# Weighted sums of an attention kernel in half groups of columns, at three places in four steps

## The chip, the cores and the metric

The kernel runs on one core of one Trainium2 chip. The core has a matrix engine (TensorE, "PE" in the profile, its weight loads "PEld"), a vector engine (VectorE, "DVE"), a scalar engine (ScalarE, "ACT"), GpSimd ("POOL") and a sync engine that issues transfers ("SP"). Matrix products go to banks of an accumulator memory of 128 partitions, 512 float32 columns each. The metric is the time of one execution on the device, in microseconds (us); lower is better. Times are medians of several executions; the profile is one execution.

## What is computed

One transformer-like block in float32 on x of 2048 rows and 512 columns. The rows are normalised; 32 query heads of 16 channels share one key and one value head; beside it stands a dense layer with Mish; the block's output is `x + s * g`.

```python
def _A_ref(x, wq, wk, wv, wo):
    q = ((x @ wq).reshape(B, S, H, Dh)).transpose(0, 2, 1, 3)
    k = x @ wk
    v = x @ wv
    scores = jnp.einsum("bhqd,bkd->bhqk", q, k) * (Dh ** -0.5)
    p = _softmax(scores, axis=-1)
    o = jnp.einsum("bhqk,bkd->bhqd", p, v)
    return o.transpose(0, 2, 1, 3).reshape(B, S, H * Dh) @ wo

def _B_ref(x, w1, b1, w2):
    h = jnp.einsum("bsd,df->bsf", x, w1) + b1
    act = h * jnp.tanh(softplus(h))
    return jnp.einsum("bsf,fd->bsd", act, w2)

xn = _layernorm(x, axis=-1)
s = _A_ref(xn, A_wq, A_wk, A_wv, A_wo)
g = _silu(_B_ref(xn, B_w1, B_b1, B_w2))
return x + s * g
```

## The kernel before

**Steps.** The attention is worked off in 512 steps. A unit `v` (there are 32) is four heads by 512 rows of queries, a block `k` (16 per unit) is 128 keys; step `s` stands for unit `s // 16`, block `s % 16`. A lead-in written as a small planner (tasks with times) does the normalisation, the keys and the first products; then the main loop runs 492 steps, and the last 20 (`LEAD`) go in pairs (`late_pair`). In the main loop each step issues to TensorE, in an order written out by hand:

- four score products `e` (`e_one`, L1098), each 64 rows of the array by 512 columns. ScalarE makes the exponential of each from the bank (L1100) into a buffer `pt`; there are `NPT` of these buffers, handed out in turn, and three banks `e`. A step fills buffers for one half of the array and two blocks, so that two neighbouring steps, an even one and the next, complete two blocks.
- four score products `m` (`m_one`, L1119) for a later unit, whose row maxima VectorE takes from the bank (L1123) into `mb`; there are three banks `m`. From the maxima `c_rows` makes the correction rows of a unit (`mp`, `cr`, once in 16 steps), which eight small transfers put beside the queries.
- half-array parts of one dense product group, `xs` in `waves` (L120, names `xps`): a group is a list of 12 or 15 products (queries, the Mish layer's first and second product, the output product), summed up in one bank.
- the weighted sum `pv` (L1187) of the block two steps back: `pv(s)` gives each of four 32-column tiles of the array its exponentials, 512 columns, with the 32-column values `vaug` as weights. It appears in the trace as eight products. After the 16th block of a unit `o_out` copies the bank out on ScalarE (L1196) and issues eight transfers.

**Halves of the array.** The products `e`, `m` and `xs` use one half of the array's rows, so that two run side by side as a pair. `waves` works a chunk of a group's products (six of twelve; eight or seven of fifteen; five where the steps allow it) first on one half `h` in one step and then on the other half in the next: a group of 12 or 15 takes four steps, or six with chunks of five. Both halves add into the same bank. `waves` keeps order between them by `cur["relay"]`: the ScalarE or VectorE instruction that was issued just behind the last x of a step; the first x of the group's next step is given a dependence on it ("other half of the bank"). A group's first step has none. After the group's last x, `finish` issues the evacuation of the bank (`xps` has one bank).

**Jobs.** The longer element-wise chains (Mish, SiLU, inverse of the softmax sums) go to ScalarE as jobs from a queue: `act_jobs(n)` issues one at the end of each step, two when over three wait, none (one when over three wait) where the step has evacuated on ScalarE. Between them GpSimd works at times counted in steps (`due`).

Of the kernel before, what the change touches and what calls it, by code (L numbers as in the profile page):

```python
# [42 lines left out]
HOLD = 1  # L43
STEP_US = 2.95
XMAX = 8
NPT = 15
EM = "MEMEMEME"
MLAG = 4
NHB = 4
# [77 lines left out]
def block_kernel(ctx: ExitStack, tc: tile.TileContext, x, wq, wk, wv, wo, w1, b1, w2, out):  # L127
# [97 lines left out]
            xin[c, tt] = sb.tile([P, D], F32, tag=tag, name=f"xin{c}_{tt}", bufs=n)  # L225
            sp.dma_start(xin[c, tt], xr[4 * c + tt])

    mvs = cp.tile([P, NKT, 2], F32, name="mvs")

    def stats(t):  # L230
        st = sb.tile([P, 6], F32, tag="st", name=f"st{t}")
        dve.bn_stats(st, xin[divmod(t, 4)])
        dve.bn_aggr(mvs[:, t], st)

    ve = cp.tile([P, NKT], F32, name="ve")
    hv = cp.tile([P, NKT], F32, name="hv")

    def stt(o, a, k, b, op0, op1):
        dve.scalar_tensor_tensor(o, a, k, b, op0=op0, op1=op1)  # L239
# [172 lines left out]
    def act_jobs(n):  # L412
        n = (int(len(jobs) > 3) if gap[0] else n) if n < 9 else n
        gap[0] = 0
        while n > 0:
            k = next((k for k, (fn, free) in enumerate(jobs)
                      if free is None or free() is not None and free() <= step[0]), None)
            if k is None:
                return
            fn = jobs[k][0]  # L420
            del jobs[k]
            fn()
            n -= 1
            ran[0] += 1
# [263 lines left out]
    def chunk_size(n, most):  # L688
        return -(-n // -(-n // most)) if n else 0

    def waves(h, em, new):

        if not cur["chunk"] and (not new or cur["g"] is None and not begin()):
            mms = []
        else:
            g = cur["g"]
            mms = cur["chunk"] or g.mms[cur["n"]:cur["n"] + chunk_size(len(g.mms) - cur["n"], g.most)]  # L700
        second = bool(cur["chunk"])
        k = len(mms)
        ms = em(k, second)
        a = deque(ms[1 - h])
        b = deque(ms[h])
        ps = cur["ps"]
        ends = second and cur["n"] + k == len(cur["g"].mms)
        xs = deque(mms)
        swap = k % 2 and k > 5 and not second
        relay = None  # L710
        first = True
        done = False
        while a or b or xs:
            if xs:
                i = xs.popleft().half(ps, h)
                if first and cur["relay"] is not None:
                    tc.add_manual_dep(i.ins, cur["relay"].ins.name, mybir.DependencyInfo(
                        mybir.DependencyClass.Sync, mybir.DependencyReason.DATA), reason="other half of the bank")
                first = False
                if ends and cur["g"].dve and len(xs) == HOLD + k % 2:  # L720
                    held[0] = []
                if not xs and ends:
                    cur["n"] += k
                    cur["chunk"] = []
                    finish()
                    done = True
                    for top in held[0] or ():
                        top()
                    held[0] = None
            elif b and not swap:  # L730
                b.popleft()()
            if len(a) > 1 or a and not xs:
                r = a.popleft()()
                if k and not xs and relay is None:
                    relay = r
            if b and swap and not xs and not a:
                b.popleft()()
        if k and not done:
            assert relay is not None
            cur["relay"] = relay  # L740
            if second:
                cur["n"] += k
                cur["chunk"] = []
            else:
                cur["chunk"] = mms
# [400 lines left out]

    def c_rows(v):

        mp = sb.tile([P, 2, 3, 8], F32R, tag="mp", name=f"mp{v}", bufs=2)
        mx = f(mp[:, :, 0])  # L1150
        w = {}

        def reduce():
            dve.reduce_max(out=mx, in_=mb_of[v].rearrange("p b (a z) -> p a z b", a=2), axis=AX.X)

        def high():
            dve.tensor_reduce(out=mp[:, :, 1], in_=mx.rearrange("p a (z o) -> p a z o", o=1), axis=AX.X,
                              op=ALU.max, negate=True)

        def low():  # L1160
            dve.tensor_reduce(out=f(mp[:, :, 2]), in_=f(mp[:, :, 0:2]).rearrange("p a s z -> p a z s"), axis=AX.X,
                              op=ALU.add, negate=True)

        def turn():
            cr = w["cr"] = sb.tile([P, 32], F32, tag="cr", name=f"cr{v}", bufs=2)
            dve.transpose(cr, f(mp[:, :, 1:3]).rearrange("p a s z -> p a (s z)"))

        def move():
            q, cr = qt_of[v], w["cr"]
            for a in range(1, -1, -1):  # L1170
                r = 64 * a + 48
                for b in range(4):
                    sp_at(0.68)
                    sp.dma_start(f(q[r:r + 2]).rearrange("o p (t b n) -> b o (p t) n", b=4, n=32)[b],
                                 cr[32 * b + 16 * a:32 * b + 16 * a + 16])
        return reduce, high, low, turn, move

    def pv(s):
        v, k = divmod(s, 16)
        if k == 0:  # L1180
            pv_of[v] = ps_v.tile([P, C], F32, tag="v", name=f"pv{v}")
        o = pv_of[v]
        for p in range(2):
            for a in range(2):
                pt = pt_of.pop((s, p, a))
                j = 2 * p + a
                pe.matmul(o[32 * j:32 * j + 32], vaug[:, k], pt, start=(k == 0), stop=(k == 15))  # L1187

    def o_out(v):
        c, g = divmod(v, 8)  # L1190
# [83 lines left out]
    def due(t):  # L1274
        step[0] = t
        for k in sorted(k for k in timed if k <= t):
            for fn in timed.pop(k):
                fn()
# [264 lines left out]
    rowq = deque()  # L1543
    pv_next = [0]

    def pv_to(s):

        while pv_next[0] <= s:
            k = pv_next[0]
            pv(k)  # L1550
            pv_next[0] += 1
            if k % 16 == 15:
                o_out(k // 16)
                return

    for s in range(NS + 2000):
        inm = s < NS - LEAD
        if inm or cur["chunk"]:
            assert s < NS
            due(s)  # L1560
            h = s % 2

            def em(k, second):
                n, rest = m_sides(1 - h, k, second) if inm else (0, 0)
                x = deque(lambda i=i: e_one(s, i) for i in range(4))
                y = deque(lambda: m_one(1 - h) for _ in range(n))
                r = [[], []]
                for op in EM if k % 2 == 0 or k == 5 or second else EM[::-1]:
                    if op == "M" and y:
                        r[1 - h].append(y.popleft())  # L1570
                    elif op == "E":
                        r[1 - h].append(x.popleft())
                r[h] = [lambda j=j: m_one(h, n + rest > 4 and j == rest - 1) for j in range(rest)]
                return r

            if s >= 2 and (s - 1) % 16 == 0 and s > 1:
                gap[0] += 1
            waves(h, em, s < NS - LEAD - 1)
            act_jobs(1 + (len(jobs) > 3))
            due(s + 0.5)  # L1580
            pv_to(s - 2)
        elif s < NS:
            due(s)
            if not late_banks:
                late_banks.extend(ps_m.tile([P, C], F32, tag="m", name=f"late{k}") for k in range(3))
                if (NS - s) % 2:
                    for i in range(4):
                        e_one(s, i)
                    fill(4)
                    act_jobs(1)  # L1590
                    pv_to(s - 2)
                    step[0] = s
                    continue
            if (NS - s) % 2 == 0:
                late_pair(s)
            else:
                if s < NS - 3:
                    act_jobs(1)
                pv_to(s - 1)
        else:  # L1600
            due(s)
            if s == NS:
                act_jobs(2)
                pv_to(NS - 1)
                due(s + 0.5)
                lanes_end()
                fill(3)
                fill(3)
            fill(16)
            act_jobs(100)  # L1610
        step[0] = s
        if vdone[0] < 8 * NC and min(m_next) >= m_need(vdone[0]):
            r = c_rows(vdone[0])
            rowq.extend([lambda r=r: (r[0](), behind.append(r[1])),
                         lambda r=r: (r[2](), behind.append(lambda: (r[3](), r[4]())))])
            vdone[0] += 1
        if rowq and not evacs[0]:
            rowq.popleft()()
        while behind and s >= NS - LEAD - 1:
            behind.popleft()()  # L1620
        evacs[0] = 0
        pump()
        if s > NS + 1 and not queue and cur["g"] is None and not timed and not jobs:
            break
# [12 lines left out]
```

## Time and profile before

| | |
|---|---|
| median of 3 runs | 1576.38 us (1576.18 to 1576.9) |
| the profiled execution | 1576.55 us |
| its span, first to last instruction | 1574.4 us |
| granted TensorE clock | 1.000 |
| instructions | 31742 |

A line of a group reads: line of the kernel, engine, operation, output<-inputs by the program's names, shape, count | busy us, mean ns of one | idle us of the engine ahead of them, and what released it. A line of a timeline reads: start in us, us taken, engine, line, operation, names, shape, count; in brackets the idle time ahead and its releaser. Consecutive instructions of one kind that overlap are merged. A matmul's duration is a latency: the next one may start earlier.

### The profile page before, as it was taken

To read this page: it belongs to the slowest core of one execution; us is meant where nothing else is said; L and a number is where in the kernel's file an instruction comes from. 1 tells how busy PE (TensorE), PEld (TensorE's weight loads), DVE (VectorE), ACT (ScalarE), POOL (GpSimd) and SP (SyncE) were. 2 spreads that over 40 slices of the span, in tenths; PEclk is the share of its full clock that TensorE was granted. 3 is DMA by queue.
4 is the path that set the end of the run, shared out by engine and by line. 5 is a ranking of instruction groups with operands and counts; after the bars stand their busy time and mean duration, and the time that the engine had idled before them with its cause. 6 is when DMAs were issued, how large, how long until landed. Compare 5 with 4: busy or idle time off the path is not lost.

```text
span 1574.4 us, 31742 instructions
## 1 busy us (share of the span) xinstructions
PE 1562.6 (99%) x11738; PEld 842.0 (53%) x11738; DVE 1341.1 (85%) x2329; ACT 1307.8 (83%) x2518; POOL 633.7 (40%) x683
## 2 busy tenths in 40 slices
PE   9999999999999999999999999999999999999998
PEld 5555555555555555555555555555555555555554
DVE  8998888889889888888998988888889998888832
ACT  7588788798998779878989887887898878789886
POOL 4774266284464105503515320471251515126412
PEclk9999999999999999999999999999999999999999
DMA  6243231232331314122032222211332213032020
GB/s 191 93 124 112 65 101 44 60 118 84 125 97 41 103 44 137 45 69 83 24 100 65 64 93 69 85 59 30 112 99 85 74 40 111 19 111 58 15 81 28
DMA packets 74666, 124.31 MB, mean 79 GB/s; under 512 B 21520, under 2 KB 35344, under 8 KB 74512
## 3 DMA queue, kind: packets, MB, share of 16 engines
q1 hardware_dynamic: 74512, 122.29, 25.2%
q8 instruction: 93, 1.52, 0.4%
q14 instruction: 61, 0.50, 0.1%
HBM read 74.78 MB, written 26.21 MB: 64 GB/s over the span
## 4 chain that ended last, share of the span: by engine, by line
PE 95%; DVE 4%; ACT 1%; DMA 0%; issue 0%; SPq 0%; ACTq 0%; DVEq 0%
PE xps L120 44%; PE pv L1187 32%; PE e L1098 9%; PE m L1119 7%; DVE mb L1123 3%; PE late L120 1%; PE xps L116 0%; ACT pt L1100 0%; DMA xin<-in_dram 0%; PE late L1098 0%; PE kp L351 0%; PE wop L120 0%; PE xp L302 0%; PE late L116 0%; PE wop L116 0%
## 5 line engine op out<-in xcount | busy, mean ns | idle before, releaser
L1123 DVE TENSOR_REDUCE mb<-m 128x1 f32<-128x512 f32 x2048 | 1274.2, 683 | 171.3 <-PE m L1119 152.3
L1100 ACT ACTIVATE pt<-e 128x512 f32<-128x512 f32 x2018 | 1061.6, 602 | 220.7 <-PE e L1098 212.3
L1119 PE MATMUL m<-ks,qt 48*128 48x512 f32 (+1 forms) x2048 | 829.9, 421 | 1.6 <-DVE ks L239 0.5
L1098 PE MATMUL e<-qt,ks 64*128 64x512 f32 x2018 | 740.4, 401 | 0.3
L1187 PE MATMUL pv<-pt,vaug 128*32 128x512 f32 x4096 | 543.0, 604 | 0.0
L1119 PEld LDWEIGHTS m<-ks,qt 48*128 48x128 f32 (+1 forms) x2048 | 372.9, 185 | 55.7 <-DVE mb L1123 18.5
L1098 PEld LDWEIGHTS e<-qt,ks 64*128 64x128 f32 x2018 | 373.3, 186 | 17.9 <-ACT pt L1100 7.5
L120 PE MATMUL xps<-wbs,act 64*128 64x512 f32 x1248 | 339.1, 408 | 0.2
L120 PEld LDWEIGHTS xps<-wbs,act 64*128 64x128 f32 x1248 | 217.7, 185 | 177.4 <-ACT pt L1100 105.8
L120 PE MATMUL xps<-xt,ws 64*128 64x512 f32 x1104 | 305.8, 410 | 0.1
L120 PEld LDWEIGHTS xps<-xt,ws 64*128 64x128 f32 x1104 | 190.6, 185 | 182.7 <-ACT pt L1100 116.5
L174 POOL TENSOR_SCALAR t<-t 128x512 f32<-128x512 f32 x56 | 34.4, 615 | 395.1 <-ACT t L838 394.9
L1187 PEld LDWEIGHTS pv<-pt,vaug 128*32 128x32 f32 x4096 | 81.9, 108 | 137.4 <-issue 129.1
L164 POOL TENSOR_TENSOR hb<-hb,t 128x512 f32<-128x512 f32 x56 | 72.1, 1287 | 65.6 <-ACT t L851 52.4
L120 PE MATMUL xps<-xt,wq 64*128 64x512 f32 x336 | 93.2, 410 | 0.0
L120 PEld LDWEIGHTS xps<-xt,wq 64*128 64x128 f32 x336 | 58.0, 185 | 55.2 <-ACT pt L1100 35.2
L120 PE MATMUL xps<-wbs,ot_all 64*128 64x512 f32 x288 | 79.5, 409 | 0.0
L120 PEld LDWEIGHTS xps<-wbs,ot_all 64*128 64x128 f32 x288 | 49.6, 185 | 46.7 <-ACT pt L1100 29.3
L164 POOL TENSOR_TENSOR hb<-hb,u 128x512 f32<-128x512 f32 x56 | 72.3, 1291 | 4.4
L164 POOL TENSOR_TENSOR u<-u,t 128x512 f32<-128x512 f32 x56 | 71.8, 1282 | 4.7
L164 POOL TENSOR_TENSOR act<-hb,act 128x512 fp32r<-128x512 f32 x55 | 70.8, 1288 | 4.6
L159 POOL TENSOR_SCALAR qh<-qf 128x512 fp32r<-128x512 f32 x15 | 9.3, 620 | 111.8 <-ACT qf L770 76.2
(158 smaller groups left out, 954.9 us busy)
## 6 DMA issues: line engine op xcount, KB each, us to landing
wbs<-w SPq DMA_DIRECT2D x36, 512.0 KB
ws<-w SPq DMA_DIRECT2D x35, 512.0 KB
qt<-qh SPq DMA_DIRECT2D x256, 32.0 KB
w<-wbs SPq DMA_DIRECT2D x14, 512.0 KB
wq<-wq SPq DMA_DIRECT2D x14, 512.0 KB
wbs<-wo SPq DMA_DIRECT2D x12, 512.0 KB
rawws<-in_dram SPq DMA_DIRECT2D x21, 256.0 KB
rawwb<-in_dram SPq DMA_DIRECT2D x20, 256.0 KB
```

The costliest lines, as they stand in the source:

```text
L120: i = self.pe.matmul(ps, self.lhs()[o], self.rhs()[o], start=(self.k == 0 and self.halves == 0), stop=(self.k == self.tot - 1 and self.hal ...
L159: pool.tensor_scalar(o, i, 1.0, 0.0, op0=ALU.mult, op1=ALU.add)
L164: eng.tensor_tensor(out=o, in0=a, in1=b, op=op)
L174: pool.tensor_scalar(o, o, lim, 0.0, op0=ALU.min, op1=ALU.max)
L1098: pe.matmul(e, ks[o:o + 64, P * k:P * (k + 1)], q[o:o + 64, p], start=True, stop=True)
L1100: r = act.activation(pt, e, AF.Exp, scale=0.25)
L1119: pe.matmul(m, q[o, p, P * t:P * (t + 1)], ks[o, C * kb:C * (kb + 1)], start=True, stop=True)
L1123: r = dve.reduce_max(out=mb_of[v][:, kb, z:z + 1], in_=m, axis=AX.X)
L1187: pe.matmul(o[32 * j:32 * j + 32], vaug[:, k], pt, start=(k == 0), stop=(k == 15))
```

## The change

The weighted sums move within the steps. `gstep` counts the steps of a group from 0. Steps with `gstep % 3 == 1` do jobs and weighted sums in the middle of the step, when half of its `xs` are out; steps with `gstep % 3 == 2`, and those that end a group or have none, do them at the end; the others do none. The position of the sums is counted in halves of 256 columns: in the middle of step `s` they go up to the first half of block `s - 2`, at the end up to all of it. A block goes whole when both halves are wanted at once, and always for the first and the last block of a unit; else it goes as two products of 256 columns, at different places. Over a group of four steps that makes one and a half blocks in the middle of the second, one and a half at the end of the third, one at the end of the fourth.

There is one more buffer for exponentials (`NPT` 16). The statistics of the rows, three small constant tiles, become one tile that shares a buffer with the Mish chain's "t"; `mp` and `cr` have one buffer instead of two.

```diff
-NPT = 15
+NPT = 16
...
-    mvs = cp.tile([P, NKT, 2], F32, name="mvs")
+    vecs = sb.tile([P, NKT, 4], F32, tag="t", name="vecs", bufs=2)
+    mvs = vecs[:, :, 0:2]
...
-    ve = cp.tile([P, NKT], F32, name="ve")
-    hv = cp.tile([P, NKT], F32, name="hv")
+    ve, hv = vecs[:, :, 2], vecs[:, :, 3]
...
-    def waves(h, em, new):
+    gstep = [0]
+
+    def waves(h, em, new, mid):
...
+        gstep[0] = 0 if not k or not second and cur["n"] == 0 else gstep[0] + 1
+        if gstep[0] % 3 != 1:
+            mid = None
         ms = em(k, second)
...
             if b and swap and not xs and not a:
                 b.popleft()()
+            if mid and len(xs) <= k // 2:
+                mid()
+                mid = None
...
-        mp = sb.tile([P, 2, 3, 8], F32R, tag="mp", name=f"mp{v}", bufs=2)
+        mp = sb.tile([P, 2, 3, 8], F32R, tag="mp", name=f"mp{v}", bufs=1)
...
-            cr = w["cr"] = sb.tile([P, 32], F32, tag="cr", name=f"cr{v}", bufs=2)
+            cr = w["cr"] = sb.tile([P, 32], F32, tag="cr", name=f"cr{v}", bufs=1)
...
-    def pv(s):
+    def pv(s, half=None):
         v, k = divmod(s, 16)
-        if k == 0:
+        if k == 0 and not half:
             pv_of[v] = ps_v.tile([P, C], F32, tag="v", name=f"pv{v}")
         o = pv_of[v]
+        z = slice(0, C) if half is None else slice(C // 2 * half, C // 2 * (half + 1))
         for p in range(2):
             for a in range(2):
-                pt = pt_of.pop((s, p, a))
+                pt = pt_of[s, p, a] if half == 0 else pt_of.pop((s, p, a))
                 j = 2 * p + a
-                pe.matmul(o[32 * j:32 * j + 32], vaug[:, k], pt, start=(k == 0), stop=(k == 15))
+                pe.matmul(o[32 * j:32 * j + 32, z], vaug[:, k], pt[:, z], start=(k == 0), stop=(k == 15))
...
-    def pv_to(s):
-
-        while pv_next[0] <= s:
-            k = pv_next[0]
-            pv(k)
-            pv_next[0] += 1
-            if k % 16 == 15:
+    def pv_halves(n):
+
+        while pv_next[0] < n:
+            k, h = divmod(pv_next[0], 2)
+            if h == 0 and (pv_next[0] + 1 < n or k % 16 in (0, 15)):
+                pv(k)
+                pv_next[0] += 2
+            else:
+                pv(k, h)
+                pv_next[0] += 1
+            if pv_next[0] % 32 == 0:
                 o_out(k // 16)
                 return
+
+    def pv_to(s):
+        pv_halves(2 * s + 2)
...
-            waves(h, em, s < NS - LEAD - 1)
-            act_jobs(1 + (len(jobs) > 3))
-            due(s + 0.5)
-            pv_to(s - 2)
+            def mid():
+                act_jobs(1 + (len(jobs) > 3))
+                pv_halves(2 * s - 3)
+
+            waves(h, em, s < NS - LEAD - 1, mid)
+            if gstep[0] % 3 == 2 or cur["g"] is None or s == NS - LEAD - 1:
+                act_jobs(1 + (len(jobs) > 3))
+                due(s + 0.5)
+                pv_halves(2 * s - 2)
+            else:
+                due(s + 0.5)
```

## The prediction

> **What bounds the kernel now.** I read the page first: the engines' shares, the clock, the chain that ended last, the costliest groups.
>
> ```profile
> PE 1562.6 (99%) x11738; PEld 842.0 (53%) x11738; DVE 1341.1 (85%) x2329; ACT 1307.8 (83%) x2518; POOL 633.7 (40%) x683
> PEclk9999999999999999999999999999999999999999
> PE 95%; DVE 4%; ACT 1%; DMA 0%; issue 0%; SPq 0%; ACTq 0%; DVEq 0%
> PE xps L120 44%; PE pv L1187 32%; PE e L1098 9%; PE m L1119 7%; DVE mb L1123 3%; PE late L120 1%; PE xps L116 0%; ACT pt L1100 0%; DMA xin<-in_dram 0%; PE late L1098 0%; PE kp L351 0%; PE wop L120 0%; PE xp L302 0%; PE late L116 0%; PE wop L116 0%
> L1123 DVE TENSOR_REDUCE mb<-m 128x1 f32<-128x512 f32 x2048 | 1274.2, 683 | 171.3 <-PE m L1119 152.3
> L1100 ACT ACTIVATE pt<-e 128x512 f32<-128x512 f32 x2018 | 1061.6, 602 | 220.7 <-PE e L1098 212.3
> ```
>
> TensorE is busy 99% of the time, at its full clock, and makes 95% of the chain; VectorE (the maxima) and ScalarE (the exponentials) each have about a sixth of the time free. So what counts is how many us of TensorE one step takes. One step in order of time, TensorE first, then the same step's exponentials (one of them alone, then all four merged) and maxima:
>
> ```profile
> 700.60 0.50 PE L120 MATMUL xps<-xt,ws 64*128 64x512 f32 x1
> 700.61 0.49 PE L1119 MATMUL m<-ks,qt 48*128 48x512 f32 x1
> 700.94 0.40 PE L1098 MATMUL e<-qt,ks 64*128 64x512 f32 x1
> ...
> 701.64 0.39 PE L1119 MATMUL m<-ks,qt 48*128 48x512 f32 x1
> 701.87 0.39 PE L120 MATMUL xps<-xt,ws 64*128 64x512 f32 x1
> 701.87 0.66 PE L1098 MATMUL e<-qt,ks 64*128 64x512 f32 x2
> 702.11 0.39 PE L1119 MATMUL m<-ks,qt 48*128 48x512 f32 x1
> 702.46 1.06 PE L1187 MATMUL pv<-pt,vaug 128*32 128x512 f32 x8
> 703.46 0.50 PE L120 MATMUL xps<-xt,ws 64*128 64x512 f32 x1
> ```
> ```profile
> 702.40 0.59 ACT L1100 ACTIVATE pt<-e 128x512 f32<-128x512 f32 x1
> ```
> ```profile
> 701.38 2.10 ACT L1100 ACTIVATE pt<-e 128x512 f32<-128x512 f32 x4 [0.79 <-PE e L1098]
> ```
> ```profile
> 701.17 2.48 DVE L1123 TENSOR_REDUCE mb<-m 128x1 f32<-128x512 f32 x4 [0.42 <-PE xps L120]
> ```
>
> A step is 703.46-700.60 = 2.86 us: seven pairs of half-array products (six x, four m, four e), then the weighted sum's eight products (pv). Pairs follow each other at 0.23 us (701.64, 701.87, 702.11), but the first after pv takes 0.34 (700.60 to 700.94), and pv starts 0.35 after the last pair. Seven pairs alone would end at 0.34+6x0.23 = 1.73.
>
> **What an insertion of pv costs.** Near the end two and three blocks stand together:
>
> ```profile
> 1516.62 1.92 PE L1187 MATMUL pv<-pt,vaug 128*32 128x512 f32 x16
> 1518.48 0.50 PE L1098 MATMUL e<-qt,ks 64*128 64x512 f32 x1
> ```
> ```profile
> 1510.93 2.78 PE L1187 MATMUL pv<-pt,vaug 128*32 128x512 f32 x24
> 1513.65 0.49 PE L1098 MATMUL late<-qt,ks 64*128 64x512 f32 x1
> ```
>
> One block: 1.00 us to the next product (702.46 to 703.46); two 1.86, three 2.72. A further block is 0.86, so an insertion costs 0.14 inside, 0.35-0.23 = 0.12 ahead and 0.34-0.23 = 0.11 behind: 0.37 us. The change takes one of four insertions out of each group of four steps. Of 492 steps (512-20) that is about 121 groups: 121x0.37 = 45 us, the gross gain.
>
> **Halves of 256 columns.** One block in a group is split: 16 products of half width for 8. The nearest row is the keys' projection, also 128x32 weights and 256 columns, followed by its weight loads:
>
> ```profile
> 30.14 1.07 PE L336 MATMUL kq<-xf,wkf 128*32 128x256 f32 x16
> 31.14 0.49 PE L1119 MATMUL m<-ks,qt 64*128 64x512 f32 x2
> ```
> ```profile
> 30.14 0.59 PEld L336 LDWEIGHTS kq<-xf,wkf 128*32 128x32 f32 x16 [0.24 <-ACT xin L211]
> ```
>
> Its 16 products take 1.00 us to the next, as 8 of full width do, the loads inside them. I take 0; the other end is loads that lie open, two more rounds at 0.59/4 = 0.15 each, 0.3 x 121 = 36 us. The Trainium skill ("TensorE: Matmul & The Clock Gate", Part 3, The mechanism) says that a weight load runs beside matmuls in flight only when its row group differs; these column tiles all use every row, so by it halves would cost near that end. The kq row, with 0.59 us of loads inside 1.00, speaks for 0.
>
> **What the removed pv covered.** Half-products of one group into one bank come first from one half of the array, in the next step from the other. `waves` therefore makes the first x of a step wait for `relay`: the ScalarE exponential issued right behind the last x of the step before (in a step of six x the third exponential). The view of waits shows it (us in total, times, longest):
>
> ```profile
> PEld xps L120 <- ACT pt L1100: 301.6, 360, 1.0
> ```
>
> 360 times, about three steps in four (a group's first step has no relay), the releaser of the first x's weights is an exponential. The gap is 0.84 us each, which is pv's time: today the wait ends under pv. Above, the third exponential runs 702.40 to 702.99, and x starts at 703.46, half a us later. Steps 0 and 1 of the whole run have no pv behind them, and there it lies open (ScalarE, then weight loads, then products):
>
> ```profile
> 83.52 0.59 ACT L1100 ACTIVATE pt<-e 128x512 f32<-128x512 f32 x1
> ```
> ```profile
> 83.44 0.18 PEld L1119 LDWEIGHTS m<-ks,qt 64*128 64x128 f32 x1 [0.20 <-DVE mb L1123]
> 84.16 0.18 PEld L120 LDWEIGHTS xps<-xt,early 64*128 64x128 f32 x1 [0.53 <-ACT pt L1100]
> 84.16 0.18 PEld L1119 LDWEIGHTS m<-ks,qt 64*128 64x128 f32 x1
> ```
>
> The exponential ends at 84.11, x follows at 84.16 (0.05 later), and the m and e behind it in TensorE's order wait with it: 0.72 us pass where pairs take 0.23.
>
> In the changed kernel the `gstep` test puts pv in the middle of step 1 (one and a half blocks), at the end of step 2 (one and a half) and at the end of step 3 (one, since the group has ended). So no pv stands between steps 0 and 1, nor between the last x of step 1 and the first of step 2.
>
> **The sum for a group of twelve products** (six x a step):
> - Step 0: the next x may start at 702.99+0.05, so the step is 2.44 us, for 1.73 of work.
> - Step 1: three pairs 0.80, 0.12 into pv, pv 1.00+0.43 = 1.43: 2.35. Then pairs x-e, x-m, x-e, m-e. The last x's e starts 0.57 in; its exponential starts 0.53 later (701.87 to 702.40), runs 0.59, 0.05 to release: 1.74, for 1.03 of work. Together 4.09.
> - Step 2: 1.86 to pv's start, 1.43: 3.29.
> - Step 3: 2.86, as now.
> Sum 12.68 for 4x2.86 = 11.44: +1.24 us. The 0.37 saved is in it.
>
> **A group of fifteen products** (eight x in two steps, seven in two):
>
> ```profile
> 158.66 0.49 PE L120 MATMUL xps<-wbs,act 64*128 64x512 f32 x1
> ...
> 160.39 0.39 PE L1098 MATMUL e<-qt,ks 64*128 64x512 f32 x1
> ...
> 161.71 0.49 PE L120 MATMUL xps<-wbs,act 64*128 64x512 f32 x1
> ```
> ```profile
> 160.89 0.60 ACT L1100 ACTIVATE pt<-e 128x512 f32<-128x512 f32 x1
> ```
>
> Here the relay is the fourth exponential, ending 161.49. Step 0: 161.54-158.66 = 2.88. Step 1: four pairs 1.03, 0.12, 1.43; then the e 0.80 in, plus 0.50+0.60+0.05: 4.53. Step 2: 3.05+0.43 = 3.48. Step 3, seven pairs: 2.86. Sum 13.75 for 3x3.05+2.86 = 12.01: +1.74.
>
> By the program's lists 32 groups have fifteen products; I take two of them as spread over six steps of five x (the program's second way), where four relays lie open and two insertions go: 2x1.24 = 2.5 each. With 30 other groups of fifteen that leaves 121-32 = 89 of twelve: 89x1.24+30x1.74+2x2.5 = 110+52+5 = 167 us.
>
> **The other parts.**
> - Sixteen buffers of exponentials, handed round in order. In step 2 of a group whose first step has an even number, exponentials three and four need the buffers filled sixteen exponentials earlier, two steps before the group; these belong to the split block and come free only with its second half, after step 2's pairs. Their start moves from 1.8 to about 2.55 into the step (1.86 + 0.43 + the tail and release); the relay then ends at 3.2, pv at 3.29: hidden in a twelve, by little. In a fifteen the fourth ends some 0.4 after pv; with two thirds of them even that is 30x2/3x0.4 = 8 us, which I add. Queued behind on ScalarE are the jobs and step 3's exponentials; two jobs there can push the group's evacuation 0.4 past the last pv, at most 0.4x80 = 32 us, an upper end.
> - ScalarE's jobs (Mish, SiLU, softmax inverses) have three places a group for four: later, but a product that needs them has two groups in between. 0; the other end is several empty steps, some 10 us.
> - The output copy and its eight SP transfers move half a step ahead, at block 15 of a row group, once in 16 steps. The copy waits for pv in front of three exponentials, whose e come after that pv anyway: 0.
> - One buffer for `mp` and `cr`: used once per 16 steps, 46 us. `vecs` takes one of two "t" buffers: the second Mish exponential must now wait for the last normalisation.
>
> ```profile
> 50.24 0.62 ACT L838 ACTIVATE t<-hb 128x512 f32<-128x512 f32 x1
> ```
> ```profile
> 50.11 0.20 POOL L275 TENSOR_TENSOR rstd<-hv,rstd 128x4 f32<-128x4 f32 x1
> ```
>
> That is 0.1 us on ScalarE, 0.5 at most.
>
> Sum: 167+8 = 175, against the profiled execution's 1576.55 us (span 1574.4; the median of the runs is 0.17 less): 1752.
>
> **The rivals.**
> - A switch saved and nothing lost (ends faster): the first x isn't held, because the exponentials run ahead. Then 1576.5-45 = 1532. For it: the 1.00/1.86/2.72 rows. Against it: the relay would have to end 0.7 us sooner in steps 0 and 1; the row at 84.16 shows it binding. It decides where exponentials end under 1.73 us after a step's start; they end at 2.39. The Trainium skill ("TensorEngine Tiling (Array Packing)", Key Properties) states that changing the tiling mode drains the engine; by that rule this rival's time would hold. The trace agrees on the drain, 0.37 us.
> - The maxima's three banks set the pace. If the relay does not bind, runs of ten and eleven pairs hold six m each. Reductions end 1.25, 1.85, 2.45 after the run's start (701.17 plus 0.68, then each 0.60 later, from 2.48 for four). The fifth m, due at 1.74, waits for 1.90, the sixth thus for 2.5 instead of 2.2: 0.3 twice a group, 0.6-0.37 = +0.23, 121x0.23 = 28: 1605. For it: the 0.20 at 83.44, where m waits for a maximum. Against it: 0.53 for the relay right behind, which gives VectorE time to catch up.
> - Relay and buffers both bind, with the 32 and 10 us above: 1752+42 = 1794, and empty steps on top.
> - That the change does nothing can't be: the order on TensorE changes in every group.
>
> **How the numbers follow.** Relay exposed, around 1752: 0.78, its own range 1715 to 1790. More of it, around 1794: 0.07. Maxima, 1605: 0.08. Plain gain, 1532: 0.07. Predicted 1752. For 8 in 10 the range is 1700 to 1805: halves with open loads (+36) and jobs above; two stalls each 0.2 us shorter (121x0.4 = 48) below. Faster by over 0.2% (about what a measurement here can tell): 0.07; within 0.2%: 0.01; slower 0.92.
>
> **What would show it.** Right: the gap of the first x in steps 1 and 2 of a group stands open with "ACT pt" as releaser, TensorE falls to some 92 to 94% busy, a group of twelve takes 12.7 us, pv has three runs a group, and the kq-like halves stay at 0.43. Wrong: steps 0 of 1.8 us (the relay ends early), m released by "DVE mb" instead (banks), or empty steps without x (jobs late).

## The result and the profile after

| | before | changed |
|---|---|---|
| median | 1576.45 us | 1766.89 us |
| ratio, 95% interval | | 1.1208 [1.1189, 1.1228] |
| span of the profiled execution | 1574.4 us | 1765.0 us |

The change costs 190 us, 12%. The prediction said 1752, between 1700 and 1805. First the page of the changed kernel (lines move by 8 or 9: the exponential is L1108, the maximum L1131, pv L1196):

```profile
PE 1610.1 (91%) x12571; PEld 885.7 (50%) x12571; DVE 1351.9 (77%) x2332; ACT 1313.9 (74%) x2517; POOL 635.0 (36%) x683
PE 72%; ACT 21%; DVE 3%; issue 2%; DMA 1%; POOL 0%; SPq 0%; ACTq 0%; POOLq 0%; DVEq 0%
PE xps L120 33%; PE pv L1196 27%; ACT pt L1108 20%; PE m L1127 5%; PE e L1106 5%; DVE mb L1131 3%; PE late L120 1%; PE xps L116 0%; ACT os L1205 0%; PE late L1106 0%; DMA xin<-in_dram 0%; PE xp L302 0%; PE kp L351 0%; POOL y L164 0%; DMA qt<-cr 0%
```

The exponentials, which had no share of the chain before, now make 20% of it, and TensorE falls from 95% to 72%. Share of busy time says less: 99% became 91%, because a matmul's recorded duration runs on into the gap behind it: in the group below the last e before 703.75 starts at 702.79, 0.96 us earlier, and only 0.48 counts as idle. Who ends the gaps is in the view of waits (us in total, times, longest). The changed kernel, then the kernel before:

```profile
PEld xps L120 <- ACT pt L1108: 296.4, 327, 1.3
PE xps L120 <- ACT pt L1108: 130.8, 236, 0.9
PEld m L1127 <- DVE mb L1131: 41.1, 85, 0.9
```
```profile
PE xps L120 <- ACT pt L1100: 0.2, 1, 0.2
```

Before, TensorE itself stood idle once for an exponential, for 0.2 us; the wait of the weights lay under pv. Now it stands idle 236 times, twice in each of some 118 groups, 0.55 us each on average. One group in order of time (TensorE, only x and pv, and the last e ahead of the first wait; brackets give the idle time ahead and its releaser):

```profile
701.28 0.50 PE L120 MATMUL xps<-xt,ws 64*128 64x512 f32 x1
...
702.55 0.39 PE L120 MATMUL xps<-xt,ws 64*128 64x512 f32 x1
...
702.79 0.48 PE L1106 MATMUL e<-qt,ks 64*128 64x512 f32 x1
703.75 0.50 PE L120 MATMUL xps<-xt,ws 64*128 64x512 f32 x1 [0.48 <-ACT pt L1108]
...
704.63 1.50 PE L1196 MATMUL pv<-pt,vaug 128*32 128x512 f32 x16
706.06 0.50 PE L120 MATMUL xps<-xt,ws 64*128 64x512 f32 x1
...
706.64 0.39 PE L120 MATMUL xps<-xt,ws 64*128 64x512 f32 x1
...
707.75 0.49 PE L120 MATMUL xps<-xt,ws 64*128 64x512 f32 x1 [0.48 <-ACT pt L1108]
...
709.68 1.50 PE L1196 MATMUL pv<-pt,vaug 128*32 128x256 f32 x16
711.11 0.50 PE L120 MATMUL xps<-xt,ws 64*128 64x512 f32 x1
...
713.02 1.06 PE L1196 MATMUL pv<-pt,vaug 128*32 128x512 f32 x8
714.02 0.50 PE L120 MATMUL xps<-xt,ws 64*128 64x512 f32 x1
```

The steps are 2.47, 4.00, 3.36 and 2.91 us, 12.74 in all; forecast were 2.44, 4.09, 3.29 and 2.86. Both open boundaries show: no pv between the x at 702.55 and the one at 703.75, and none between 706.64 and 707.75. A run of pv with a half in it takes 1.43 to the next product (704.63 to 706.06 and 709.68 to 711.11), as forecast.

### The profile page after: what moved, and what is told of

The parts are those of the page before. It is cut to its first block, busy times and chain, and to the rows that moved or that the text cites. A ratio compares the mean times of both kernels' runs of the same rounds, so it can differ in the third digit from the quotient of the medians.

```text
span 1765.0 us, 33610 instructions
## 1 busy us (share of the span) xinstructions
PE 1610.1 (91%) x12571; PEld 885.7 (50%) x12571; DVE 1351.9 (77%) x2332; ACT 1313.9 (74%) x2517; POOL 635.0 (36%) x683
## 4 chain that ended last, share of the span: by engine, by line
PE 72%; ACT 21%; DVE 3%; issue 2%; DMA 1%; POOL 0%; SPq 0%; ACTq 0%; POOLq 0%; DVEq 0%
PE xps L120 33%; PE pv L1196 27%; ACT pt L1108 20%; PE m L1127 5%; PE e L1106 5%; DVE mb L1131 3%; PE late L120 1%; PE xps L116 0%; ACT os L1205 0%; PE late L1106 0%; DMA xin<-in_dram 0%; PE xp L302 0%; PE kp L351 0%; POOL y L164 0%; DMA qt<-cr 0%
## 5 line engine op out<-in xcount | busy, mean ns | idle before, releaser
L1131 DVE TENSOR_REDUCE mb<-m 128x1 f32<-128x512 f32 x2048 | 1285.0, 684 | 337.9 <-PE m L1127 295.7
L1108 ACT ACTIVATE pt<-e 128x512 f32<-128x512 f32 x2016 | 1066.8, 603 | 377.8 <-PE e L1106 343.4
L1106 PE MATMUL e<-qt,ks 64*128 64x512 f32 x2016 | 756.2, 411 | 1.5 <-DMA qt<-cr 1.2
L1196 PE MATMUL pv<-pt,vaug 128*32 128x512 f32 (+1 forms) x4968 | 519.2, 525 | 0.0
L120 PE MATMUL xps<-wbs,act 64*128 64x512 f32 x1188 | 333.0, 410 | 56.7 <-ACT pt L1108 56.7
L120 PE MATMUL xps<-xt,ws 64*128 64x512 f32 x1104 | 317.3, 413 | 43.7 <-ACT pt L1108 43.3
L120 PEld LDWEIGHTS xps<-wbs,act 64*128 64x128 f32 x1188 | 203.8, 185 | 203.1 <-ACT pt L1108 97.7
L1196 PEld LDWEIGHTS pv<-pt,vaug 128*32 128x32 f32 x4968 | 122.3, 108 | 206.4 <-issue 178.8
L164 POOL TENSOR_TENSOR oc<-oc,sc 128x512 f32<-128x512 f32 (+1 forms) x16 | 20.7, 1291 | 125.6 <-ACT sc L1224 98.9
```

The costliest lines, as they stand in the source:

```text
L120: i = self.pe.matmul(ps, self.lhs()[o], self.rhs()[o], start=(self.k == 0 and self.halves == 0), stop=(self.k == self.tot - 1 and self.hal ...
L164: eng.tensor_tensor(out=o, in0=a, in1=b, op=op)
L1106: pe.matmul(e, ks[o:o + 64, P * k:P * (k + 1)], q[o:o + 64, p], start=True, stop=True)
L1108: r = act.activation(pt, e, AF.Exp, scale=0.25)
L1131: r = dve.reduce_max(out=mb_of[v][:, kb, z:z + 1], in_=m, axis=AX.X)
L1196: pe.matmul(o[32 * j:32 * j + 32, z], vaug[:, k], pt[:, z], start=(k == 0), stop=(k == 15))
```

## The experiments

Theory A is the prediction's: pv used to cover the wait of a step's first x for the relay, and two of these waits now lie open. Rivals: B, the three banks of the maxima pace longer runs of pairs; C, only the number of insertions counts. Before had a median of 1576.2 to 1576.3 us beside these runs.

**1. Only take the cover away.** The kernel before; one block of a group moves from the end of its second step to the middle. Insertions, whole blocks, buffers and job places stay.

```diff
+        gstep[0] = 0 if not k or not second and cur["n"] == 0 else gstep[0] + 1
+        if gstep[0] != 1:
+            mid = None
...
+            if mid and len(xs) <= k // 2:
+                mid()
+                mid = None
...
-            waves(h, em, s < NS - LEAD - 1)
+            waves(h, em, s < NS - LEAD - 1, lambda: pv_to(s - 2))
```

> The kernel before, with one thing changed: in the second step of each group the weighted sum (one whole block) stands in the middle of the step instead of at its end. Four insertions per group as before, no halves, 15 buffers, jobs where they were. Theory A (the pv covered the wait for the relay): the boundary between the second and the third step lies open; +0.71 us in each of 89 groups of twelve, +0.92 in 30 of fifteen, about +1 in the rest, 92 us in all: 1668 us, and the first x of the third step waits for the exponential. Theory B (three banks of the maxima pace longer runs of pairs): eleven pairs in a row, +0.3 x 121 = 36 us: 1612, the m waiting for VectorE. Theory C (only the number of insertions counts): 1576.

Measured 1683.27 us, ratio 1.0678 [1.0647, 1.0709]. Weight loads, ScalarE and waits of this kernel:

```profile
760.34 0.19 PEld L1106 LDWEIGHTS e<-qt,ks 64*128 64x128 f32 x1
761.43 0.18 PEld L120 LDWEIGHTS xps<-xt,wq 64*128 64x128 f32 x1 [0.91 <-ACT pt L1108]
```
```profile
760.79 1.08 ACT L1108 ACTIVATE pt<-e 128x512 f32<-128x512 f32 x2
```
```profile
PE xps L120 <- ACT pt L1108: 67.7, 119, 0.8
```

119 open boundaries, half as many as in the changed kernel, and half its idle time (67.7 of 130.8). The exponential that starts at 760.79 takes 0.59 and ends at 761.38; x follows at 761.43. B (1612) and C (1576) are out. Most of the 15 us above A's sum are groups of twelve at 12.28 us on average (+0.84, for +0.71): single ones take 12.15, and half of the rest lies in the third step, whose pv comes later (2.92 us for 2.85 before). Why it does wasn't looked into.

**2. Shorten the relay.** The changed kernel, with a copy of one column on ScalarE right behind the last x in the relay's place:

```diff
+                if not xs and not ends:
+                    relay = act.activation(turns[:, 0:1], one, AF.Copy)
+                    tc.add_manual_dep(relay.ins, i.ins.name, SYNC, reason="half of the bank")
```

> The changed kernel, with the relay shortened: right behind the last x of a step ScalarE issues a copy of one column that waits for that x, and the next step's first x waits for this copy instead of the exponential behind it. Theory A: the copy ends about 1.98 us after the step's start (it queues behind the second exponential, 1.78, and is taken as 0.2) where the third exponential ended at 2.39, so each open boundary loses 0.4 of its 0.7 us: 0.84 per group, 119 groups, -100 us: 1667. Theory B (banks): the copy changes nothing about the maxima, 1767. If the relay were no cause: 1767 or a little more for the extra ScalarE work.

Measured 1672.8 us, ratio 1.0611 [1.0569, 1.0653]: 94 us less than the changed kernel, for the 100 expected. ScalarE, weight loads and waits:

```profile
863.12 0.20 ACT L728 ACTIVATE turns<-one 128x1 f32<-128x1 f32 x1
```
```profile
863.37 0.18 PEld L120 LDWEIGHTS xps<-wbs,act 64*128 64x128 f32 x1 [0.40 <-ACT turns L728]
```
```profile
PE xps L120 <- ACT turns L728: 23.5, 69, 0.5
PEld m L1130 <- DVE mb L1134: 59.5, 165, 0.8
```

TensorE's idle time ahead of x falls from 130.8 to 23.5 us. The edit also changes something that isn't meant: the separate semaphore instructions ahead of a step's first exponential, which experiments 6 to 8 are about, fall from 364 to 11 in the compiled program. The places tell the two apart. In groups of twelve the time from the last pair to the next x falls from 0.96 to 0.54 us at the first open boundary and from 0.87 to 0.50 at the second; with the groups of fifteen that alone sums to 93 us. Where those instructions go with nothing else but one buffer (experiment 8), the two times together stay as they were (0.93 and 0.90). So shortening the wait for the relay, without removing it, gives back about half of the 190 us by itself. As it shrinks, m waits for the maxima more often (165 times for 85): rival B's limit is the next one.

**3. One open boundary instead of two.** The changed kernel, the second step's sums at its end:

```diff
-        if gstep[0] % 3 != 1:
-            mid = None
+        mid = None
...
-            if gstep[0] % 3 == 2 or cur["g"] is None or s == NS - LEAD - 1:
+            if gstep[0] % 3 or cur["g"] is None or s == NS - LEAD - 1:
```

> The changed kernel, with the second step's sums at its end instead of its middle, whole blocks only: two blocks at the end of the second step, one at the end of the third and of the fourth. Three insertions as in the changed kernel. Theory A: only the boundary between first and second step lies open. A group of twelve 2.44+3.72+2.86+2.86 = 11.88 (+0.44 to before), one of fifteen 2.88+3.92+3.05+2.86 = 12.71 (+0.70): 65 us, 1641, and some 10 more for steps without products. Theory B alone (no relay): 14 pairs in a row with eight m, the last due at 3.13 but held to 3.7: +0.6-0.37 = +0.23, 1605. Theory C: 1532.

Measured 1672.27 us, ratio 1.0608 [1.0577, 1.0639]. This kernel's wait:

```profile
PE xps L120 <- ACT pt L1107: 66.8, 119, 0.9
```

119 waits again, one a group. The time is 20 us over A's 1651, and the experiments on jobs and buffers below say where most of that lies (16 and about 11, against the 10 allowed). An insertion is saved here too, and does not pay for one open boundary.

**4. Without halves in the changed kernel.**

```diff
-                pv_halves(2 * s - 3)
+                pv_halves(2 * s - 2)
```

> The changed kernel without halves: the middle of the second step takes two whole blocks, the ends of the third and fourth one each. Theory A: the same two boundaries lie open, the same sum of 12.68 for a group of twelve; the split block's buffers come free earlier, so exponentials three and four of the third step no longer wait for them: -0.27 in a group of fifteen, 8 us: 1759. If halves cost by themselves (their weight loads open, 0.3 us a group) 36 us go as well: 1723.

Measured 1769.47 us, ratio 1.1225 [1.1192, 1.1257]: no gain. Groups of fifteen take 13.99 us in the median, as in the changed kernel. So neither halves cost anything nor does the split block's late release: that term of the prediction, 8 us, doesn't exist as it was put.

**5. Halves alone, in the kernel before.**

```diff
-            pv(k)
+            if k % 16 in (0, 15):
+                pv(k)
+            else:
+                pv(k, 0)
+                pv(k, 1)
             pv_next[0] += 1
```

> The kernel before, with every block but the first and last of a unit given as two halves of 256 columns, one right behind the other at the old place. Prices the halves alone, on some 430 blocks. By the row of the keys' projection (16 half products in 1.00 us, as 8 whole ones): 1576.4, no change. If each further round of weight loads lay open (0.3 us a block): +129, 1705.

Measured 1579.02 us, ratio 1.0013 [1.0004, 1.0023]. Its page:

```profile
PE 1564.5 (99%) x15322; PEld 959.3 (61%) x15322; DVE 1341.4 (85%) x2329; ACT 1308.6 (83%) x2518; POOL 635.0 (40%) x683
```

One block with its loads and the next x:

```profile
700.30 1.07 PE L1188 MATMUL pv<-pt,vaug 128*32 128x256 f32 x16
701.30 0.50 PE L120 MATMUL xps<-xt,ws 64*128 64x512 f32 x1
```
```profile
700.29 0.59 PEld L1188 LDWEIGHTS pv<-pt,vaug 128*32 128x32 f32 x16 [0.24 <-issue]
```

3584 more products and weight loads (15322 for 11738), eight for each of 448 blocks, cost under 3 us, 0.006 a block. The loads (0.59 us) lie inside the 1.00 us of the products, although all four column tiles use every row of the array; the row of the keys' projection was the right price. The rule of the Trainium skill ("TensorE: Matmul & The Clock Gate", Part 3, The mechanism) that a load runs beside matmuls only in other row groups isn't what is measured here; the same section also lets a load into a background weight buffer run ahead, and no run here shows whether that is what happens.

**6. The memory part alone, in the kernel before**: 16 buffers, the statistics in a "t" buffer, one `mp` and one `cr`.

```diff
-NPT = 15
+NPT = 16
...
+    vecs = sb.tile([P, NKT, 4], F32, tag="t", name="vecs", bufs=2)
...
-        mp = sb.tile([P, 2, 3, 8], F32R, tag="mp", name=f"mp{v}", bufs=2)
+        mp = sb.tile([P, 2, 3, 8], F32R, tag="mp", name=f"mp{v}", bufs=1)
```

> The kernel before with only the memory part of the change: 16 buffers of exponentials, the statistics in one of the two t buffers, one buffer for the correction rows. Expected 1576.5: 0.1 us on ScalarE at 50 us, nothing on TensorE. If the shared buffer held the lead-in up: up to 1577.

Measured 1590.1 us, ratio 1.0078 [1.0056, 1.0101]. A miss: 14 us from a part that was priced at 0.1. The groups of the main loop are longer by 0.14 us throughout (11.57 for 11.43), nothing at the start. Each step's pv starts later after the last pair, 0.378 instead of 0.349 us in the median of 491 steps: 491 x 0.029 = 14.2 us.

Where that comes from is in the list of waits on semaphores in the compiled program. An exponential waits for TensorE; some also for an earlier exponential. With 15 buffers these are 212 second ones of a step (and six others), with 16 it is 270 first ones (and 58 third). Theory D: such an exponential gets a separate semaphore instruction ahead of it; when that hits the first exponential of a step, the fourth e, which needs that exponential's bank, comes later, and pv behind it.

**7. Another number of buffers, nothing else.** 14 has the same pattern as 16 (271 first ones).

```diff
-NPT = 15
+NPT = 14
```

> The kernel before with 14 buffers of exponentials instead of 15 and nothing else. In the program's list of waits 212 exponentials carry a second semaphore with 15 buffers, all but a few the second of their step; with 16 (the run of the memory part alone) it is 270 times the first, with 14 it is 271 times the first. Theory D: a second semaphore is a separate instruction ahead of the exponential (0.05 to 0.06 us); ahead of the first exponential it delays the fourth e, which waits for that bank, and so pv. Then 14 buffers cost what 16 did, about +14: 1590, and pv starts 0.38 instead of 0.35 after the last pair. If the memory moves or the number of buffers did it: 1576.

Measured 1590.34 us, ratio 1.0087 [1.007, 1.0103], the time of the memory part alone. So it isn't the memory moves, and not one buffer more or less as such. Two steps in a row of this kernel, ScalarE and then weight loads:

```profile
715.91 2.06 ACT L1100 ACTIVATE pt<-e 128x512 f32<-128x512 f32 x4 [0.27 <-PE e L1098]
...
718.77 1.57 ACT L1100 ACTIVATE pt<-e 128x512 f32<-128x512 f32 x3 [0.28 <-PE e L1098]
```
```profile
715.07 0.18 PEld L120 LDWEIGHTS xps<-xt,wq 64*128 64x128 f32 x1 [0.84 <-ACT hb L830]
...
716.57 0.18 PEld L1098 LDWEIGHTS e<-qt,ks 64*128 64x128 f32 x1
717.00 0.16 PEld L1187 LDWEIGHTS pv<-pt,vaug 128*32 128x32 f32 x8 [0.25 <-issue]
717.99 0.18 PEld L120 LDWEIGHTS xps<-xt,wq 64*128 64x128 f32 x1 [0.84 <-ACT pt L1100]
...
719.42 0.18 PEld L1098 LDWEIGHTS e<-qt,ks 64*128 64x128 f32 x1
719.84 0.16 PEld L1187 LDWEIGHTS pv<-pt,vaug 128*32 128x32 f32 x8 [0.24 <-issue]
```

The first of the two has the semaphore instruction ahead of its first exponential, the second doesn't. Counted from the step's first x, the first exponential starts at 0.84 in the one step and 0.78 in the other, the last e's load at 1.50 and 1.43, pv at 1.93 and 1.85. The whole trace says the same: of 356 steps of six x, 186 have the instruction; their first exponential starts at 0.84, their pv 0.41 after the last pair (medians), in the other 170 it is 0.78 and 0.35. In both kinds the fourth e's weights load 0.05 after that exponential's end. In steps of eight x, where the fourth e comes later, pv starts 0.32 after the last pair with the instruction and without it. Within one trace neither memory nor the number of buffers differs, so theory D holds.

**8. The changed kernel with 15 buffers** (`NPT = 15`).

> The changed kernel with 15 buffers of exponentials instead of 16. The second semaphore stands ahead of the first exponential 5 times instead of 364. Theory D: two steps of a group (third and fourth) get their pv 0.05 us sooner, about 0.1 x 120 = 12 to 15 us: 1753. If fewer buffers hold the third step's last exponential long enough to delay the fourth step: 1767 or more.

Measured 1756.17 us, ratio 1.1139 [1.1117, 1.1161]: 10.7 us under the changed kernel. The sixteenth buffer isn't needed for speed, and costs.

**9. A fourth place for jobs** in the changed kernel, at the end of a group's first step.

```diff
             else:
+                if gstep[0] % 3 == 0:
+                    act_jobs(1 + (len(jobs) > 3))
                 due(s + 0.5)
```

> The changed kernel with a fourth place for jobs, at the end of each group's first step. Groups of the changed kernel have 17 empty steps (no product ready) where before had 2, and its end after the main loop is 8 us longer. If the three places for jobs cause them: empty steps fall to about 2 and the time by about 10 us, 1757. If they come from elsewhere: 1767, 17 empty steps still.

Measured 1750.56 us, ratio 1.1096 [1.1056, 1.1135]: 16.3 us less, and between the groups the trace has two empty steps (no product ready) again for 17. With a quarter fewer places for jobs products were not ready in time, presumably because the Mish chains ended later, and the work went to the end: from the end of the main loop to the end of the span it is 81.0 us in the changed kernel, 66.5 before and 66.6 here. That is 14 us longer, where the expectation said 8, and nearly all of the 16.3.

**10. All of it together.** Sums at step ends, the short relay, the fourth place.

```diff
-        if gstep[0] % 3 != 1:
-            mid = None
+        mid = None
...
+                if not xs and not ends:
+                    relay = act.activation(turns[:, 0:1], one, AF.Copy)
...
-            if gstep[0] % 3 == 2 or cur["g"] is None or s == NS - LEAD - 1:
+            if gstep[0] % 3 or cur["g"] is None or s == NS - LEAD - 1:
...
             else:
+                act_jobs(1 + (len(jobs) > 3))
                 due(s + 0.5)
```

> Sums at step ends (two blocks, one, one), relay shortened by the one-column copy, and the fourth place for jobs, all in one: does what was found add up, and does three insertions pay once the wait is short? From 1672 for the step ends: one open boundary shortened by 0.4 x 119 = 48, the jobs 10: 1614. If it comes under 1576 the saved insertion pays; if it stays near 1614, the three banks of the maxima over 14 pairs (held 0.6 by rival B) are what is left, 0.23 to 0.3 a group.

Measured 1636.04 us, ratio 1.037 [1.0333, 1.0407], 22 us over the 1614 expected. Three insertions don't pay even so. Waits of this kernel:

```profile
PEld m L1129 <- DVE mb L1133: 58.6, 187, 0.8
PE xps L120 <- ACT turns L727: 11.6, 30, 0.6
```

The relay's idle time is down to 11.6 us; m waits for maxima 187 times (56 before). That fits rival B as the next limit, and the steps show it. In groups of twelve the first step falls from 2.49 us in experiment 3 to 2.04 with the short relay, but the second, pairs eight to fourteen of a run without pv, rises from 3.70 to 4.13: an m in it is released by a maximum in all 89 such steps (10 of 88 in experiment 3). So almost all that the short relay gives, the three banks of the maxima take back. Of the 60 us that remain over before, some 37 lie in these second steps; the first ones still wait 0.52 us from the last pair to the next x, where pairs take 0.23.

**11. Another order of e and m in the kernel before**, to start the first exponential sooner.

```diff
-EM = "MEMEMEME"
+EM = "EMEMEMEM"
```

> The kernel before with the order of a step's products turned, e ahead of m (EMEMEMEM for MEMEMEME, where x are even in number). Theory D says that the fourth e, which waits for the first exponential, sets pv's start in the kernel before too: with the first e a pair (0.23 us) sooner pv would start 0.32 instead of 0.35 after the last pair, -0.03 x 490 = -14 us, 1562. Against it: the maxima start a pair later, and VectorE is busy 85%; if that decides, 1576 or more.

Measured 1635.06 us, ratio 1.038 [1.0362, 1.0398], the wrong way. The instruction behind the last x is now an m, so that the relay becomes its maximum on VectorE. In steps of eight x it ends after pv; two of these:

```profile
PEld xps L120 <- DVE mb L1123: 303.7, 345, 1.2
```
```profile
701.60 0.18 PEld L120 LDWEIGHTS xps<-wbs,act 64*128 64x128 f32 x1 [1.10 <-DVE mb L1123]
...
705.01 0.18 PEld L120 LDWEIGHTS xps<-wbs,act 64*128 64x128 f32 x1 [1.19 <-DVE mb L1123]
```

Gaps of 1.10 and 1.19 us where 0.84 is pv's own: with pv in its old place, too, a relay that ends later than pv lies open, as A says. From pv to the next x these 59 steps take 1.27 us for 1.00 before, 16 us in all. In the 354 steps of six x the wait stays covered (1.00 as before). These lose 0.10 us each, 36 us, ahead of pv: the first exponential does start sooner (0.57 for 0.78 after the step's first x), yet pv starts 0.43 after the last pair, where 0.35 was measured before and 0.32 expected. The fourth e doesn't wait for that exponential here (its weights load 0.36 us after the exponential's end, 0.05 in the kernel before), so the run doesn't test theory D. m waits for maxima 394 times (56 before); that this holds the step up would fit rival B, and isn't shown.

**12. The short relay in the kernel before.**

> The kernel before with the shortened relay of the second experiment. The relay ends under pv anyway, so theory A expects nothing of it: 1576, within 3 us for the extra 0.2 us of ScalarE in three steps of four. A gain of tens of us would mean that the relay costs something even where pv covers it.

The edit is that of the second experiment. Measured 1575.08 us, ratio 0.9991 [0.9981, 1.0]: under cover the relay's length costs nothing. The same edit that was worth 94 us in the changed kernel is worth about 1 here.

## Why the prediction was right

- **Bound and insertions.** An insertion at 0.37 us and contiguous blocks at 0.86: pv runs of the changed kernel take 1.43 and 1.00 to the next product. Right.
- **Halves at 0.** Right: +2.7 us for 448 blocks.
- **The relay, two open boundaries a group.** Right in place, number and size. From a group's first x to the next group's, 78 groups of twelve without an empty step take 12.80 us on average (before 11.43), 27 of fifteen take 14.06 (before 12.20). That is +1.36 and +1.86 for +1.24 and +1.74; the surplus of 0.12 is about what 16 buffers add: with 15 (experiment 8) they take 12.70 and 14.01 us.
- **The step "sixteen buffers, split block late": 8 us.** It failed; without halves nothing is gained, and with it goes the rival at 1794, which rested on more of the same. Buffers do cost, by another way: 16 makes the second semaphore fall on a step's first exponential, 10.7 us here and 14 in the kernel before. The prediction had looked for a buffer that comes too late, not for where a wait is placed.
- **The step "jobs: 0, the other end some 10 us".** The term was missized: 16.3 us, with 15 more empty steps and 14 us more work behind the main loop. The prediction had named empty steps as a sign of being wrong, and they came.
- **`vecs`, `mp`, `cr`: nothing.** Right; 14 buffers without these moves give the same time as 16 with them.

Taking jobs and buffers out, 1766.9-16.3-10.7 leaves 1739.9, 163 us over before; the relay's sum was 167. (The two edits weren't run together, and they overlap a little: the fourth place also brings the semaphore instructions ahead of first exponentials from 364 to 270. By their share of the 10.7 us that is an estimated 3 us counted twice.) So the point came out 15 us low because 27 us of two small terms stood against 8 assumed; and as those 8 were for something that doesn't happen, it was luck that they brought the point nearer.

- **The rivals.** The plain gain (1532) had the right price for an insertion and the wrong cover; the rule of the Trainium skill on mode changes ("TensorEngine Tiling (Array Packing)", Key Properties) fits the 0.37 us of an insertion, though no run shows a drain apart from other costs of an insertion, and doesn't decide. The banks (1605) didn't decide while the relay did; they show once it is short. TensorE's busy share was put at 92 to 94%, and is 91%.

## What to carry to other kernels

Before work is moved that looks like pure overhead, list the waits that end while it runs: here 0.37 us of switching also hid a wait for another engine, 360 times, that added 0.6 to 0.9 us where the change laid it open. A dependence that only orders two products should hang on something short and early; whichever instruction happens to follow is a moving target, as the turned order of e and m showed in its long steps. And shortening one wait can hand the pace to the next, here the banks of the maxima. A number of buffers in turn is also an alignment: 14 and 16, for four uses a step, cost 14 us where 15 cost none.

## What was not expected of the hardware

- A second semaphore ahead of an exponential delays it by 0.06 us (0.84 for 0.78 from the step's start). Ahead of the second exponential of a step that is free, ahead of the first it moves pv by 0.06 in steps of six x, 14 us in all; in steps of eight x that is free, too.
- 16 products of 256 columns on four column tiles, each with its own weight load, take the time of 8 of 512 (0.006 us a block more), the loads (0.59 us) inside the products' 1.00 although they use the same rows.
- A copy of one column on ScalarE takes 0.20 us by its record, and the product that waits for it is released 0.25 after the copy's start (863.12 to 863.37). With an exponential in its place it is 0.64 (760.79 to 761.43).
